# Raw W1 tiles loaded into later W2 places, and two weights' low parts subtracted on VectorE

## The chip, the cores and the metric

The kernel runs on one core of one Trainium2 chip. The metric is the device time of one execution in microseconds; the kernel before takes 933.64 us, the median of three runs (932.16 to 934.44). One more execution was profiled, and all rows of this document's first part come from it.

## The reference

Inputs are x (8 batches, 8 heads, 512 tokens, 64 features) and state (8, 8, 32, 64). Three stages follow each other.

```
a  = softmax(x @ state^T / 8);  xread = a @ state          # 512 rows a batch
a2 = softmax(state @ x^T / 8);  sread = a2 @ x             # 32 rows a batch
x1 = [xread ; sread], heads side by side                   # 8 x 544 x 512
x2 = x1 + relu(layernorm(x1) * g @ W1) @ W2                # W1 512x2048, W2 2048x512
out = (sigmoid(causal_conv5(x2)) * (x2 @ w_val)) @ w_out   # two weights of 512x512
```

The weights come as 64-bit floats and are turned into 32-bit ones on the chip.

## The kernel before, in words

**Precision.** A product of 32-bit numbers is made of three fp32r matmuls: each operand is split into a high part and a low part (`split_sb`, L72: ScalarE copies the high part at L73, and the engine given as an argument subtracts it from the source at L74), and `mm3` (L76 to L79) adds high by low, low by high and high by high. For the first four tiles of the hidden layer in batch 0 plain fp32 matmuls are used instead (L601, L639).

**Weights.** W1 is cut into 16 tiles `("1", j)`, four for each quarter q = j // 4 of the hidden layer, and W2 into 16 tiles `("2", f)`, one for each block of 128 hidden features. A raw tile is 128 x 512 numbers of 8 bytes, 4 KB in a partition. `load_raw` (L446 to L449) issues its DMA on SyncE's queue. `decode_a` (two ScalarE activations, L463 and L465) and `decode_b` (four VectorE instructions, L471, L473, L474, L478) make a 32-bit tile of it. A W2 tile, raw and later split into two parts, lives in a place of its own, `w2_0` to `w2_15`, 4 KB each. Raw W1 tiles go through four rotating buffers, `raw`, so a fifth can only be loaded when one of the first four has been decoded. The plain copies of W2 tiles 0 to 3 stand in the places w2_15 and w2_14 for a while, so the raw tiles 14 and 15 are loaded late (L814).

**Order.** TensorE's order is the program's. On ScalarE, VectorE, GpSimd and SyncE the order from about 28 us on is chosen when the kernel is built, by a scheduler that keeps its own reckoning of time: of the instructions that are ready by this reckoning it takes the one with the lowest priority number. The loads stand at the head of the program (L794 to L813) in the order W1 tiles 0 and 1, x of batch 0, W1 tiles 2 and 3, W2 tiles 0 and 1, state of batch 1, then `order[2:8]`, then x of batch 1 and so on. `order` (L783) is the order of decoding:

```
order = [("2", 0), ("2", 1), ("1", 4), ("2", 2), ("1", 5), ("1", 6), ("2", 3), ("1", 7)]
```

`share` (L947) deals the tiles of `order` out over the blocks f of the loop `segment` (L570): W1 tile 6 belongs to f = 2, W1 tile 7 and the four splits `("s", 0..3)` (L524, L525) to f = 3, W2 tiles 4 and 5 to f = 4. `behind` (L454) adds an edge of order: a tile that is dealt out at block f has its ScalarE part after the relu (L624) of block f - 1, and the splits `("s", j)` come after the last instruction of W1 tile 7.

**What W1 tiles 4 to 7 are for.** After the plain matmuls of block f = 3, TensorE makes the column sums of W1's second quarter: `colsum_parts(1)` (L156, eight matmuls, two for each of the W1 tiles 4 to 7), a ScalarE copy (L161), `colsum(1)` (L169), a copy (L170). Then `m_steps(0, 1)` (L138) multiplies the states by these W1 tiles, VectorE adds a correction (L144) and splits the result (L74), and from block 4 on the hidden layer is computed from that (`mm<-ahl,m`).

**The last phase's weights.** `prep_weights` (L773) loads, decodes and splits w_val during batch 2 (L896) and w_out while the state rows go through the hidden layer (L902), with `decode_split` (L484).

Of the kernel before, what the change touches and what calls it, by code (L numbers as in the profile page):

```python
# [44 lines left out]
def tile_kernel(ctx: ExitStack, tc: tile.TileContext, xT, xk, stT, sn, w1, w2, wval, wout, convw, gln, ident, out):  # L45
    nc = tc.nc
# [8 lines left out]
    def sb(shape, dt, tag, bufs=1):  # L55
        cnt[0] += 1
        return main.tile(shape, dt, tag=tag, bufs=BUFS.get(tag, bufs), name=f"{tag}_{cnt[0]}")
# [14 lines left out]
    def split_sb(hi, lo, src, eng):  # L72
        nc.scalar.activation(hi, src, AF.Copy)  # L73
        eng.tensor_tensor(lo, src, hi.bitcast(F32), op=ALU.subtract)  # L74
# [371 lines left out]
    def load_raw(tag, src):  # L446
        r = sb([P, DM, 2], U32, tag)
        nc.sync.dma_start(out=r, in_=src.bitcast(U32).rearrange("p (n two) -> p n two", two=2))
        return r  # L449
# [30 lines left out]
    def decode(r, c):  # L480
        decode_a(r, c)
        decode_b(r, c)

    def decode_split(tag, r):  # L484
        c = sb([P, DM], F32, "c")
        decode(r, c)
        hl = sb([P, 2, DM], F32R, tag)
        split_sb(hl[:, 0], hl[:, 1], c, nc.gpsimd)
        return hl

    raws, plain_w2 = {}, {}
# [281 lines left out]
    def prep_weights(src, dst, tags):  # L773
        for k in range(KT):
            raw = load_raw(tags[k], src[k * P:(k + 1) * P, :])
            dst[k] = decode_split(tags[k], raw)
            yield
# [9 lines left out]

    def load_tile(kind, j):
        if kind == "1":
            raws["1", j] = load_raw("raw", w1[j // 4, j % 4])  # L790
        else:
            raws["2", j] = load_raw(f"w2_{j}", w2[j * P:(j + 1) * P, :])

    load_tile("1", 0)  # L794
    load_state(0, nc.scalar)
    load_tile("1", 1)
    load_x(0)
    nc.scalar.dma_start(out=g_sb.rearrange("p k o -> p (k o)"), in_=gln)
    for j in range(2, KT):
        load_tile("1", j)  # L800
# [214 lines left out]
```

## Time and profile before

| | us |
|---|---|
| median of 3 runs | 933.64 |
| profiled execution | 934.39 |
| its span, first to last instruction | 932.6 |
| TensorE busy in it | 909.9 |
| VectorE / ScalarE / GpSimd busy | 579.5 / 375.7 / 191.8 |

The span is what the rows cover; 1.8 us of the profiled execution's time lies around it. TensorE is the engine with the least idle time, so what counts for the end is where it stands idle or runs at the lower of its two clock levels. Idle time on another engine matters only where TensorE waits for that engine.

### The profile page before, as it was taken

To read this page: it belongs to the slowest core of one execution; us is meant where nothing else is said; L and a number is where in the kernel's file an instruction comes from. 1 tells how busy PE (TensorE), PEld (TensorE's weight loads), DVE (VectorE), ACT (ScalarE), POOL (GpSimd) and SP (SyncE) were. 2 spreads that over 40 slices of the span, in tenths; PEclk is the share of its full clock that TensorE was granted. 3 is DMA by queue.
4 is the path that set the end of the run, shared out by engine and by line. 5 is a ranking of instruction groups with operands and counts; after the bars stand their busy time and mean duration, and the time that the engine had idled before them with its cause. 6 is when DMAs were issued, how large, how long until landed. Compare 5 with 4: busy or idle time off the path is not lost.

```text
span 932.6 us, 12963 instructions
## 1 busy us (share of the span) xinstructions
PE 909.9 (98%) x5152; PEld 688.8 (74%) x5152; DVE 579.5 (62%) x996; ACT 375.7 (40%) x688; POOL 191.8 (21%) x163
## 2 busy tenths in 40 slices
PE   7988999999999999999999999999999999999998
PEld 2336667777777677777777777777788988888886
DVE  6788898485275663435437245342349889988871
ACT  4745574243244342314224133231326555545532
POOL 0000010011312622411341141241202022333200
PEclk8979999999999999999999999999999999999999
DMA  9912320022012111110111110110112113222122
GB/s 361 355 55 105 101 72 1 1 93 96 1 49 95 71 48 49 49 44 6 49 48 45 49 46 1 24 49 1 46 57 79 53 40 126 100 92 91 46 89 69
DMA packets 26668, 66.45 MB, mean 71 GB/s; under 512 B 10864, under 2 KB 13040, under 8 KB 22512
## 3 DMA queue, kind: packets, MB, share of 16 engines
q1 hardware_dynamic: 25984, 65.24, 19.7%
q8 instruction: 40, 0.66, 0.3%
q10 hardware_dynamic: 624, 0.40, 0.2%
q14 instruction: 20, 0.16, 0.1%
HBM read 47.80 MB, written 17.83 MB: 70 GB/s over the span
## 4 chain that ended last, share of the span: by engine, by line
PE 90%; DVE 5%; DMA 2%; ACT 1%; issue 1%; SPq 0%; ACTq 0%; DVEq 0%
PE acc L77 16%; PE acc L79 15%; PE acc L78 15%; PE mm L77 9%; PE mm L79 8%; PE mm L78 8%; PE at L138 4%; PE at L77 2%; PE at L78 2%; PE at L79 2%; PE mm L913 1%; PE acc L639 1%; PE at L385 1%; DMA big<-in_xT 1%; PE mm L601 1%; PE at L276 1%
## 5 line engine op out<-in xcount | busy, mean ns | idle before, releaser
L626 DVE SCALAR_TENSOR_TENSOR hid<-mm,hid 128x512 fp32r<-128x512 f32 (+1 forms) x140 | 92.2, 659 | 211.7 <-ACT hid L624 211.6
L77 PE MATMUL acc<-hid,w 128*128 128x512 f32 (+1 forms) x560 | 213.5, 381 | 3.2 <-DVE hid L626 2.1
L79 PE MATMUL acc<-hid,w 128*128 128x512 f32 (+1 forms) x560 | 211.5, 378 | 0.0
L78 PE MATMUL acc<-hid,w 128*128 128x512 f32 (+1 forms) x560 | 211.2, 377 | 0.0
L624 ACT ACTIVATE hid<-mm 128x512 fp32r<-128x512 f32 (+2 forms) x144 | 82.5, 573 | 245.3 <-PE mm L79 240.8
L77 PEld LDWEIGHTS acc<-hid,w 128*128 128x128 f32 x560 | 105.4, 188 | 25.6 <-DVE hid L626 2.7
L77 PE MATMUL mm<-ahl,m 128*128 128x512 f32 (+1 forms) x312 | 121.2, 388 | 0.0
L79 PEld LDWEIGHTS acc<-hid,w 128*128 128x128 f32 x560 | 105.4, 188 | 20.0
L78 PEld LDWEIGHTS acc<-hid,w 128*128 128x128 f32 x560 | 105.4, 188 | 19.2
L78 PE MATMUL mm<-ahl,m 128*128 128x512 f32 (+1 forms) x312 | 115.3, 370 | 0.0
L79 PE MATMUL mm<-ahl,m 128*128 128x512 f32 (+1 forms) x312 | 115.3, 370 | 0.0
L74 POOL TENSOR_TENSOR m<-mb,m 128x512 fp32r<-128x512 f32 x48 | 65.4, 1378 | 201.9 <-ACT m L73 201.9
L702 DVE SCALAR_TENSOR_TENSOR ahl<-big,cw,ahl 128x511 f32<-128x511 f32 (+3 forms) x128 | 103.3, 851 | 0.4
L77 PEld LDWEIGHTS mm<-ahl,m 128*128 128x128 f32 x312 | 59.0, 189 | 40.3 <-issue 32.3
L73 ACT ACTIVATE m<-mb 128x512 fp32r<-128x512 f32 x62 | 39.0, 629 | 87.6 <-DVE mb L144 87.4
L79 PEld LDWEIGHTS mm<-ahl,m 128*128 128x128 f32 x312 | 59.0, 189 | 10.2
L78 PEld LDWEIGHTS mm<-ahl,m 128*128 128x128 f32 x312 | 59.2, 190 | 8.5 <-DVE m L74 0.5
L144 DVE SCALAR_TENSOR_TENSOR mb<-cs,sbn,at 128x512 f32<-128x512 f32 x62 | 43.5, 743 | 28.8 <-PE at L138 28.8
L688 POOL TENSOR_TENSOR w<-big,w 128x512 fp32r<-128x512 f32 x24 | 38.4, 1629 | 93.6 <-ACT w L686 77.0
L78 PE MATMUL acc<-w,raw 128*128 128x512 f32 (+1 forms) x144 | 54.3, 377 | 0.0
L79 PE MATMUL acc<-w,raw 128*128 128x512 f32 (+1 forms) x144 | 54.3, 377 | 0.0
L77 PE MATMUL acc<-w,raw 128*128 128x512 f32 (+1 forms) x144 | 54.3, 377 | 0.0
(173 smaller groups left out, 1330.2 us busy)
## 6 DMA issues: line engine op xcount, KB each, us to landing
raw<-in_w SPq DMA_DIRECT2D x16, 512.0 KB, 5.2
big<-in_xT SPq DMA_DIRECT2D x8, 1024.0 KB, 5.2
w<-in_w SPq DMA_DIRECT2D x16, 512.0 KB, 9.4
big<-in_xk SPq DMA_DIRECT2D x8, 1024.0 KB, 5.7
x2d<-x SPq DMA_DIRECT2D x8, 1024.0 KB, 4.0
big<-x2d SPq DMA_DIRECT2D x8, 1024.0 KB, 4.9
out<-hid SPq DMA_DIRECT2D x16, 512.0 KB, 2.8
raw<-in_wval SPq DMA_DIRECT2D x4, 512.0 KB, 3.5
```

The source lines that it names most:

```text
L73: nc.scalar.activation(hi, src, AF.Copy)
L74: eng.tensor_tensor(lo, src, hi.bitcast(F32), op=ALU.subtract)
L77: nc.tensor.matmul(acc, lhsT=wh, rhs=xl, start=first, stop=False)
L78: nc.tensor.matmul(acc, lhsT=wl, rhs=xh, start=False, stop=False)
L79: nc.tensor.matmul(acc, lhsT=wh, rhs=xh, start=False, stop=last)
L138: nc.tensor.matmul(mp[u][32 * p:32 * p + 32, :], lhsT=stg[r, p, :], rhs=w1s[4 * q + p][r], start=True, stop=True)
L144: a = nc.vector.scalar_tensor_tensor(mb, cs[:, q], sbn[:, u], mp[u], op0=ALU.mult, op1=ALU.add)
L276: nc.tensor.matmul(sr[r, u, :], lhsT=a2T[u][:, c, r], rhs=xn[:, c, 2 * p + u, :], start=(c == 0), stop=(c == 3))
L624: marks["act"] = nc.scalar.activation(hid[:, 0], h, AF.Relu)
L626: marks["dve"] = nc.vector.scalar_tensor_tensor(hid[:, 1], h, 0.0, hid[:, 0].bitcast(F32), op0=ALU.max, op1=ALU.subtract)
L688: nc.gpsimd.tensor_tensor(lo, src, hi.bitcast(F32), op=ALU.subtract)
L702: t = nc.vector.scalar_tensor_tensor(g[:, j:], x[:, :n - j], cw_sb[:, k, PAD - j:TAPS - j], g[:, j:], op0=ALU.mult, op1=ALU.add)
```

## The change

Raw W1 tiles 4 to 7 are loaded into the places of W2 tiles 10 to 13 and no longer into the four `raw` buffers. The loads of W2 tiles 10 to 13 then use these places after W1 tiles 4 to 7 have been decoded, and W1 tiles 8 to 11 take over the `raw` buffers from tiles 0 to 3. In `decode_split` the subtraction that makes the low part of a tile of w_val and w_out goes from GpSimd to VectorE: eight instructions of 128 x 512.

```diff
         hl = sb([P, 2, DM], F32R, tag)
-        split_sb(hl[:, 0], hl[:, 1], c, nc.gpsimd)
+        split_sb(hl[:, 0], hl[:, 1], c, nc.vector)
         return hl
 ...
         if kind == "1":
-            raws["1", j] = load_raw("raw", w1[j // 4, j % 4])
+            tag = f"w2_{j + 6}" if j // 4 == 1 else "raw"
+            raws["1", j] = load_raw(tag, w1[j // 4, j % 4])
         else:
             raws["2", j] = load_raw(f"w2_{j}", w2[j * P:(j + 1) * P, :])
```

## Rows read from the trace of the kernel before

**Rows 1.** The page: busy us (share of the span) x instructions of each engine.

```profile
PE 909.9 (98%) x5152; PEld 688.8 (74%) x5152; DVE 579.5 (62%) x996; ACT 375.7 (40%) x688; POOL 191.8 (21%) x163
```

**Rows 2.** Waits of TensorE: who waited for whom, us in total, times, longest.

```profile
PE at L156 <- DVE w L478: 4.7, 1, 4.7
...
PE at L138 <- ACT t L245: 1.8, 1, 1.8
...
PE acc L77 <- DVE x L312: 1.1, 1, 1.1
```

**Rows 3.** Busy time by stretch: PE, PEld, DVE, ACT, POOL, clock, DMA share, GB/s.

```profile
14.00:28.00 14.00, 14.00 (x64) 5.64 (x63) 13.65 (x34) 7.91 (x17) 0.00 (x0) 0.97 1.02 413
...
45.50:50.10 4.60, 0.00 (x0) 0.00 (x0) 2.21 (x5) 2.86 (x6) 0.00 (x0) 0.87 0.25 100
50.10:57.40 7.30, 6.59 (x21) 1.12 (x21) 7.24 (x14) 1.74 (x3) 0.00 (x0) 0.50 0.45 144
57.40:61.40 4.00, 4.00 (x14) 1.79 (x9) 3.81 (x6) 1.93 (x4) 0.00 (x0) 0.78 0.00 0
...
100.00:140.00 40.00, 38.41 (x242) 27.23 (x242) 39.93 (x83) 25.41 (x47) 3.35 (x1) 1.00 0.26 84
```

**Rows 4.** Timeline of TensorE: start, us, instruction, count, idle before and releaser.

```profile
44.35 1.06 PE L156 MATMUL at<-w,g 128*32 128x512 f32 x6
...
63.18 0.40 PE L77 MATMUL mm<-ahl,m 128*128 128x512 f32 x1
```

**Rows 5.** Timeline of ScalarE, 44 to 53 us, and one row of 108 us.

```profile
44.46 0.60 ACT L624 ACTIVATE hid<-mm 128x512 f32<-128x512 f32 x1 [2.22 <-PE mm L601]
44.95 0.66 ACT L463 ACTIVATE c<-w 128x512 f32<-128x512 f32 x1
...
47.15 0.64 ACT L463 ACTIVATE w<-raw 128x512 f32<-128x512 f32 x1
...
52.09 0.59 ACT L161 COPY t<-at 128x512 f32<-128x512 f32 x1 [3.73 <-PE at L156]
...
108.31 0.66 ACT L463 ACTIVATE c<-w 128x512 f32<-128x512 f32 x1
```

**Rows 6.** Timeline of VectorE, 41 to 64 us.

```profile
41.70 0.43 DVE L471 TENSOR_SCALAR w<-w 128x512 f32<-128x512 f32 x1 [1.81 <-ACT w L463]
...
47.82 0.43 DVE L471 TENSOR_SCALAR w<-w 128x512 f32<-128x512 f32 x1 [3.86 <-ACT w L463]
...
60.11 1.29 DVE L74 TENSOR_TENSOR m<-mb,m 128x512 fp32r<-128x512 f32 x2
63.38 2.48 DVE L367 TENSOR_TENSOR t<-x,at 128x512 f32<-128x512 f32 x4 [1.99 <-PE at L79]
```

**Rows 7.** SyncE's queue: start, us from first to last issue, DMA, count.

```profile
17.33 10.42 SPq L448 DMA_DIRECT2D w<-in_w  x7
...
30.05 9.18 SPq L448 DMA_DIRECT2D raw<-in_w  x4
```

**Rows 8.** DMA issues between 30.0 and 30.2 us: count, KB each, us to landing.

```profile
raw<-in_w SPq DMA_DIRECT2D x1, 512.0 KB, 10.4
```

**Rows 9.** Busy time in the stretches where w_val and w_out are decoded.

```profile
290.00:313.00 23.00, 21.87 (x121) 16.02 (x120) 19.23 (x27) 11.15 (x21) 13.92 (x10) 1.00 0.29 104
700.00:720.00 20.00, 17.93 (x147) 17.52 (x146) 17.85 (x30) 13.09 (x27) 6.15 (x6) 1.00 0.22 79
```

**Rows 10.** Groups by line and shape, whole span: count | busy us, mean ns | idle before.

```profile
L474 DVE TENSOR_SCALAR raw<-raw 128x512 uint16<-128x512 uint16 x20 | 16.6, 832 | 0.3
...
L74 DVE TENSOR_TENSOR w<-c,w 128x512 fp32r<-128x512 f32 x12 | 8.2, 690 | 0.2 <-ACT w L73 0.2
L74 POOL TENSOR_TENSOR w<-c,w 128x512 fp32r<-128x512 f32 x4 | 5.8, 1452 | 11.3 <-ACT w L73 11.3
L74 POOL TENSOR_TENSOR raw<-c,raw 128x512 fp32r<-128x512 f32 x4 | 5.2, 1294 | 5.0 <-ACT raw L73 5.0
```

**Rows 11.** The same for VectorE between 288 and 314 us.

```profile
L474 DVE TENSOR_SCALAR raw<-raw 128x512 uint16<-128x512 uint16 x4 | 4.7, 1187 | 0.3
```

## The prediction, made before the change was run

> **What bounds the kernel now.** The page comes first: TensorE is busy 909.9 us of a span of 932.6 [rows 1], so 22.7 us are idle, and only those, and what runs at the lower clock, can be won. The list of TensorE's waits says where: the longest single wait is 4.7 us, at L156 on VectorE's L478, the last instruction of a weight's decode [rows 2]. The timeline places it: six of the eight column-sum matmuls run at 44.35, and the last two start only at about 50.1 [rows 4], because W1 tile 7 is not decoded. The busy times by stretch give the second price: TensorE does nothing from 45.5 to 50.1, and afterwards its granted clock is 0.50 from 50.1 to 57.4 (the lower level, 1.2 GHz) and 0.78 on average to 61.4 [rows 3]. Half of 6.59 busy us and 0.22 of 4.00 are 3.3 + 0.9 = 4.2 us lost to the clock. With the 4.6 idle before, 8.8 us hang on this place; with the short wait for L161 behind it (0.7, what 50.1 to 57.4 holds beside the 6.59 busy) it is 9.5.
>
> Why is tile 7 late? SyncE's queue shows seven W2 loads from 17.33 on, and the four raw W1 loads only from 30.05 [rows 7]; the first of these took 10.4 us to land [rows 8]. By the order of decoding that is W1 tile 6 (two raw W1 loads went before), so it was in place at 40.5, and tile 7, the next, at about 41. W1 tiles 4 to 7 want buffers that W1 tiles 0 to 3 still hold, and the scheduler lets loads with a free place pass them. VectorE shows the effect: idle 1.81 us before 41.70 and 3.86 us before 47.82, both for ScalarE's L463, which opens the decode of tiles 6 and 7 [rows 6]. ScalarE itself stood idle for 2.22 us before the relu at 44.46, then did four instructions for W2 tiles 4 and 5, and took tile 7 at 47.15 [rows 5]. So the last stretch of the delay is the order chosen at build time, by a reckoning in which tile 7 lands late; the 41 us above is when it really landed.
>
> **The change part by part.** *Places.* W2 places 10 to 13 are free from the start, so the loads of W1 tiles 4 to 7 need no wait and go out in program order. Up to and with W1 tile 7 that is twelve weight tiles of 0.524 MB, x at 1.05 MB and some 0.26 MB of small loads: 7.6 MB. At the 413 GB/s of the stretch 14 to 28 [rows 3] it takes 18.4 us, so tile 7 lands near 20 us instead of 41. That hides both idle times of VectorE. The tile's ScalarE part may then follow the relu of block f = 2 and not that of f = 3, and fits into the 2.22 idle us.
>
> What starts next is bounded in two ways. First by VectorE: its work up to the low parts of m, which end at 61.40 (60.11 + 1.29), is the same, less the 1.81 + 3.86 = 5.67 us of idling: 55.7. The hidden layer's block 4 then starts at 55.7 and not at 63.18 [rows 4], a gain of 7.4. Second by ScalarE: if the four instructions for W2 tiles 4 and 5, which have the better priority, still go ahead of the copy L161, this copy comes at 47.15 instead of 52.09 [rows 5]. If all behind it keeps its pace, low clock included (2.4 us of idling stay), the gain is 4.9. The upper end is the 9.5 from above, if L161 goes first and the correction L144 is put ahead of W2's decode. I take 6.2, the middle of 4.9 and 7.4: the ScalarE order is the one the rows show, but a shorter pause should give back some of the clock.
>
> What is late next: VectorE, which works without a pause right behind this place, so that the 1.8 us wait at L138 for L245 [rows 2] stays and moves along. From 100 to 140 us VectorE is busy 39.93 of 40 us while TensorE is 38.41 [rows 3]. Both come to this stretch earlier by the same amount, so I cost it at nothing; if VectorE gained less than TensorE, the 1.6 idle us of TensorE there would grow by the difference, at most the 7.4 - 4.9 = 2.5 us between the two bounds.
>
> *Waits added.* The loads of W2 tiles 10 to 13 now wait for the decode of W1 tiles 4 to 7, and W1 tiles 8 to 11 for tiles 0 to 3. Behind these on SyncE's queue stand x and keys of batch 1, later W1 tiles and states. The last of the decodes ends by about 45; a load takes 10.4 us when the queues are full, so W2 tile 13 is there by 56 at the latest. The next W2 tiles after 7 go through ScalarE at 108.31 [rows 5], so 50 us cover it: 0. Were this cover gone, each tile would cost up to 10.4.
>
> *Low parts on VectorE.* Eight subtractions of 690 ns go to VectorE, 5.5 us, and eight leave GpSimd, 5.2 + 5.8 = 11.0 us [rows 10]. Four lie between 290 and 313, where VectorE has 23 - 19.23 = 3.8 us free, four between 700 and 720 with 2.15 free [rows 9]; each group needs 2.8. For w_val the bounds are -1.1 (the wait at L312 [rows 2], should a VectorE that GpSimd slows less arrive earlier) and +2.8 (all four ahead of an instruction TensorE waits for). For w_out they are 0, as TensorE has no such wait there, and +2.8. I take 0 for both, the row of idle time being nearest: the free time or the end of GpSimd's interference holds them, and the tiles are not used before the last phase.
>
> In the stretch of w_val GpSimd is busy 13.92 of 23 us [rows 9], and VectorE's L474 takes 1187 ns on average against 832 over all twenty [rows 10, 11], so the two engines do slow each other. The Trainium skill, "SBUF — State Buffer", section "Who interferes with whom", speaks against the edit: a VectorE instruction with two SBUF inputs and a GpSimd instruction that reads SBUF exclude each other, and the later waits in full. The moved subtraction has two SBUF inputs, and batch 2's other GpSimd work stays, so by this rule each of the four could take 0.7 + 1.3 = 2.0 us as an estimate, 8.0 in all, against 2.8 by the rows; as the four GpSimd instructions that go blocked VectorE in turn, both sums net out near 0 for TensorE.
>
> *Sum.* 934.39 - 6.2 + 0 = 928.2 for the profiled execution; it lies 0.75 above the median of 933.64, so the median goes to 927.4.
>
> **The rivals.** *The order stays.* If the scheduler keeps tile 7 behind the relu at 44.46, it takes at best the slot of 44.95 instead of 47.15 [rows 5]: 2.2 us less, 931.4, a quarter of a per cent. For it: the delay's last stretch was order, not landing. Against it: tile 7 has the better priority, and 2.22 idle us lie open before that relu. This is also the case in which the loads come early and nothing uses it.
>
> *All of it comes back.* L161 first, full clock, no pause: 9.5, 924.1. Against it: VectorE's work allows 7.4 unless its order changes too.
>
> *Slower.* The moved subtraction waits on VectorE for ScalarE's high part, with the relu's low part (L626) queued behind it and TensorE waiting for that. Between decode and the high part's end lie 0.6 to about 3 us, as ScalarE's place for it is also chosen by a reckoning. At 1.5 us for each of eight places, with nothing hidden, it is 12 us, less 6.2: +5.8, 939.4; from 0.8 us a place on it eats the gain, from 1.2 the kernel is slower beyond what can be told. For it: VectorE has under 4 us free in either stretch [rows 9]. Against it: the twelve W2 splits already done this way had 0.2 us of idling in all before them, for ScalarE [rows 10].
>
> **How the numbers follow.** A measurement of this kernel tells 0.3%, 2.8 us, from no change. The forecast (gain 4.9 to 7.4, less or more by up to 1 for the second edit) has 0.55, all of it back 0.16, the order stays 0.18, slower 0.11. The order's 931.4 is within 0.3%. So faster 0.71, same 0.18, slower 0.11. The likeliest case reaches from 925.2 to 929.8; the range takes in the 924.1 case with a little room and the order's: 923.5 to 933.0, leaving out the slower case and the ends of the others.
>
> **What would show it.** Right: raw W1 loads 4 to 7 leave SyncE before 20 us; VectorE has no idle time over 1 us between 28 and 46; the wait of L156 on L478 is gone; a shorter one at L169 on L161 stands in its place, the clock's low stretch is shorter, and block 4's first `mm<-ahl,m` starts near 57. The stretches 290 to 313 and 700 to 720, moved by about 6 us, keep TensorE's idle time. Wrong: L463 of tile 7 still follows the relu of f = 3; the shift at block 4 is there but gone by 160 us, which would mean that VectorE's full stretch sets the end; or new waits of TensorE on L626 in the two late stretches.

## The result and the profile after

The changed kernel takes 925.47 us, the median of four runs (925.15 to 925.79), against 934.04 for the kernel before: 8.57 us less, a ratio of 0.9909 with a 95% interval of 0.9893 to 0.9926. Its profiled execution took 925.42 us with a span of 923.6. Forecast were 927.4, in a range of 923.5 to 933.0.

The list of TensorE's waits of the changed kernel, the answer to [rows 2]. The 4.7 us at L156 have become 0.3; a wait of 1.1 at L169 and one of 0.8 before block 4 stand in their place.

```profile
PE at L138 <- ACT t L245: 2.0, 1, 2.0
PE acc L77 <- DVE x L312: 1.8, 2, 1.4
...
PE at L169 <- ACT t L161: 1.1, 1, 1.1
PE at L77 <- DVE mb L144: 0.8, 1, 0.8
...
PE at L156 <- DVE w L478: 0.3, 1, 0.3
```

The queues and engines around that place, one fence each. SyncE's queue, against [rows 7]: six loads leave in one go from 9.19, among them W1 tiles 4 to 7, and the last two land 7.5 us after their issue (second fence), so tile 7 is there by 22.3 and not by 41.

```profile
9.19 5.57 SPq L448 DMA_DIRECT2D w<-in_w  x6
```

```profile
w<-in_w SPq DMA_DIRECT2D x2, 512.0 KB, 7.5
```

ScalarE, against [rows 5]: tile 7 (L463 at 42.52) now stands ahead of the relu of 44.27 and right behind that of 42.04; the four instructions for W2 tiles 4 and 5 still go ahead of the copy L161.

```profile
42.04 0.58 ACT L624 ACTIVATE hid<-mm 128x512 f32<-128x512 f32 x1
42.52 0.66 ACT L463 ACTIVATE w<-w 128x512 f32<-128x512 f32 x1
...
44.27 0.60 ACT L624 ACTIVATE hid<-mm 128x512 f32<-128x512 f32 x1 [0.49 <-PE mm L601]
44.76 0.68 ACT L463 ACTIVATE c<-w 128x512 f32<-128x512 f32 x1
...
47.03 0.57 ACT L161 COPY t<-at 128x512 f32<-128x512 f32 x1
```

VectorE, against [rows 6]: one idle time of 1.80 is left of two that summed to 5.67.

```profile
43.21 0.43 DVE L471 TENSOR_SCALAR w<-w 128x512 f32<-128x512 f32 x1 [1.80 <-ACT w L463]
...
55.57 1.35 DVE L74 TENSOR_TENSOR m<-mb,m 128x512 fp32r<-128x512 f32 x2
56.84 2.48 DVE L367 TENSOR_TENSOR t<-x,at 128x512 f32<-128x512 f32 x4
```

TensorE, against [rows 4], and the clock, against [rows 3]: block 4 starts at 56.43 and not at 63.18, and the stretch behind the column sums runs at a granted clock of 1.00 where it was 0.50.

```profile
45.54 1.05 PE L156 MATMUL at<-w,g 128*32 128x512 f32 x2 [0.32 <-DVE w L478]
47.65 1.12 PE L169 MATMUL at<-t,part 128*128 128x512 f32 x2 [1.06 <-ACT t L161]
...
56.43 0.40 PE L77 MATMUL mm<-ahl,m 128*128 128x512 f32 x1
```

```profile
47.60:54.90 7.30, 6.52 (x26) 2.05 (x26) 7.14 (x15) 1.82 (x3) 0.00 (x0) 1.00 0.32 105
```

To see where the rest came from, TensorE's order being that of the program, the start of the same matmul is subtracted in two timelines. The table gives this lead over the kernel before, in us, for its profiled execution and those of all runs below. A column names a matmul and its time in the kernel before: the first of the column sums, the first of batch 1's scores (L189), and L385, which recurs through the whole run.

| | column sums, 44 | scores of batch 1, 68 | L385, 93 | L385, 143 | L385, 300 | L385, 380 | L385, 691 | L385, 741 |
|---|---|---|---|---|---|---|---|---|
| changed kernel | 0.19 | 6.74 | 6.79 | 8.07 | 8.06 | 7.34 | 7.34 | 8.96 |
| x1_places | 0.61 | 7.01 | 8.45 | 9.42 | 9.46 | 9.47 | 9.47 | 9.80 |
| x2_low | 0.49 | 0.80 | 0.80 | 1.36 | 1.35 | 0.65 | 0.65 | 1.94 |
| x3_wout | 0.37 | 6.73 | 8.23 | 9.50 | 9.49 | 9.51 | 9.51 | 11.30 |
| x4_fill | 0.47 | 3.99 | 2.88 | 3.91 | 3.90 | 3.92 | 3.92 | 4.93 |
| x5_two | -0.57 | 5.99 | 5.93 | 7.12 | 7.18 | 7.19 | 7.19 | 7.17 |
| x6_order | 0.60 | 3.79 | 1.25 | 2.51 | 2.46 | 2.47 | 2.48 | 2.45 |
| x7_share | -0.48 | 7.50 | 4.55 | 5.59 | 5.64 | 5.63 | 5.63 | 6.93 |
| x8_fill2 | 0.21 | 6.59 | 8.05 | 9.04 | 9.03 | 9.02 | 9.02 | 11.20 |
| x9_after | 0.31 | 6.69 | 6.55 | 7.82 | 7.83 | 7.12 | 7.13 | 8.99 |
| x10_wout | -1.21 | 5.34 | 5.38 | 6.64 | 6.66 | 6.67 | 6.67 | 8.01 |
| x11_x1d | 0.36 | 1.43 | 2.42 | 3.68 | 3.67 | 3.66 | 3.67 | 3.69 |
| x12_copies | 0.47 | 6.87 | 8.34 | 9.59 | 9.58 | 8.96 | 8.96 | 10.36 |

For the changed kernel it reads: +6.55 at W1 tile 7, +1.28 between 93 and 143, -0.72 where w_val is decoded, +1.62 where w_out is. The 9.0 of the spans are these four and the 0.2 of the start.

### The profile page after: what moved, and what is told of

It reads as the page before. It is cut to its first block, busy times and chain, and to the rows that moved or that the text cites. A ratio compares the mean times of both kernels' runs of the same rounds, so it can differ in the third digit from the quotient of the medians.

```text
span 923.6 us, 12956 instructions
## 1 busy us (share of the span) xinstructions
PE 905.1 (98%) x5151; PEld 687.6 (74%) x5152; DVE 579.0 (63%) x1004; ACT 374.7 (41%) x688; POOL 179.8 (19%) x155
## 4 chain that ended last, share of the span: by engine, by line
PE 89%; DVE 5%; ACT 3%; DMA 2%; issue 1%; SPq 0%; ACTq 0%; DVEq 0%
PE acc L77 16%; PE acc L79 16%; PE acc L78 16%; PE mm L77 9%; PE mm L79 8%; PE mm L78 8%; PE at L138 4%; PE at L77 2%; PE at L78 2%; PE at L79 2%; PE mm L914 1%; PE at L276 1%; PE at L385 1%; DMA big<-in_xT 1%; PE at L262 1%
## 5 line engine op out<-in xcount | busy, mean ns | idle before, releaser
L626 DVE SCALAR_TENSOR_TENSOR hid<-mm,hid 128x512 fp32r<-128x512 f32 (+1 forms) x140 | 92.3, 659 | 210.1 <-ACT hid L624 210.0
L702 DVE SCALAR_TENSOR_TENSOR ahl<-big,cw,ahl 128x508 f32<-128x508 f32 (+3 forms) x128 | 102.8, 852 | 0.2
L144 DVE SCALAR_TENSOR_TENSOR mb<-cs,sbn,at 128x512 f32<-128x512 f32 x62 | 43.5, 743 | 28.3 <-PE at L138 27.5
```

The lines of the kernel that those rows point to most:

```text
L144: a = nc.vector.scalar_tensor_tensor(mb, cs[:, q], sbn[:, u], mp[u], op0=ALU.mult, op1=ALU.add)
L626: marks["dve"] = nc.vector.scalar_tensor_tensor(hid[:, 1], h, 0.0, hid[:, 0].bitcast(F32), op0=ALU.max, op1=ALU.subtract)
L702: t = nc.vector.scalar_tensor_tensor(g[:, j:], x[:, :n - j], cw_sb[:, k, PAD - j:TAPS - j], g[:, j:], op0=ALU.mult, op1=ALU.add)
```

## The experiments

Each was timed beside the kernel before on the same chip.

| | median us | runs | ratio to before, 95% interval |
|---|---|---|---|
| x1_places | 926.53 | 6 | 0.9930 (0.9914 to 0.9947) |
| x2_low | 932.40 | 12 | 0.9989 (0.9974 to 1.0004) |
| x3_wout | 923.08 | 4 | 0.9896 (0.9880 to 0.9911) |
| x4_fill | 929.42 | 5 | 0.9963 (0.9949 to 0.9977) |
| x5_two | 926.41 | 5 | 0.9921 (0.9909 to 0.9933) |
| x6_order | 933.30 | 12 | 0.9987 (0.9974 to 1.0001) |
| x7_share | 927.27 | 5 | 0.9929 (0.9916 to 0.9942) |
| x8_fill2 | 924.26 | 4 | 0.9896 (0.9883 to 0.9909) |
| x9_after (the changed kernel) | 925.58 | 6 | 0.9919 (0.9898 to 0.9940) |
| x10_wout (x3_wout) | 924.72 | 6 | 0.9907 (0.9885 to 0.9929) |
| x11_x1d | 931.11 | 12 | 0.9985 (0.9968 to 1.0002) |
| x12_copies | 924.54 | 6 | 0.9912 (0.9889 to 0.9935) |

**The two edits apart.** x1_places leaves `decode_split` on GpSimd:

> Only the places of the raw W1 tiles 4 to 7 are changed; the low parts of w_val and w_out stay on GpSimd. Theory P (the places carry nearly all of the gain): the profile keeps the lead of 8.1 us that the changed kernel had at the column sums of batch 2 (6.55 from W1 tile 7, 1.34 from the writes of x1 that leave earlier, 0.2 from the start) up to the end, so about 8 us under the kernel before: 926. Theory L (the subtractions matter as much): it is 2 us or more slower than the changed kernel, 927.5 or above.

x2_low is the other half, the kernel before with `nc.vector` in `decode_split`:

> Only the eight subtractions go to VectorE; the places stay as before. Theory P: a loss of 0.7 us near 310 (w_val, TensorE waits longer for the copy at L312) and a gain of 1.6 near 715 (w_out, TensorE's wait of 1.75 for L626 goes), 0.9 us in all: 933.1. Theory L: 2 us or more, 932 or below. The prediction's own term was 0, 934.0.

Measured are 6.9 us for the places (933.40 to 926.53) and about 1.0 for the subtractions, whose interval reaches 1. x1_places keeps its lead between L385 at 300 and 380, and x2_low loses 0.70 there and gains 1.29 from 691 to 741, much as the changed kernel does (-0.72 and +1.62). Theory P holds. About 0.3 of the 1.62 is not the subtractions' doing: x1_places, which has them on GpSimd, gains 0.33 there, and x4_fill (below), which has them there too, even 1.01.

x3_wout takes the better half of the second edit:

```diff
-        split_sb(hl[:, 0], hl[:, 1], c, nc.vector)
+        split_sb(hl[:, 0], hl[:, 1], c, nc.gpsimd if tag == "raw" else nc.vector)
```

> Places changed, w_out's four subtractions on VectorE, w_val's four left on GpSimd. If the w_val part costs 0.7 us, this one is 0.7 us faster than the changed kernel: 924.8, TensorE's waits on L312 near 303 sum to 1.1 and not to 1.8. If that loss was chance of one execution, it is the same, 925.5.

923.08, more than expected. The lead over 300 to 380 no longer falls, which is w_val's 0.7; another 1.5 us come between the scores of batch 1 and L385 at 93, where the code is the same. x9_after and x10_wout are the two kernels again, on one chip:

> The changed kernel once more, beside the version with w_val's low parts on GpSimd. If the difference between the two so far (925.5 against 923.1) was w_val's 0.7 us and for the rest chance between occasions, it now lies within 1.2 us of that version; if w_val's subtractions cost more than the 0.7 that the traces show, the difference stays above 2.

> Places changed, w_out on VectorE, w_val on GpSimd, once more: 0.7 us faster than the changed kernel on the same chip, by w_val; 2 us or more faster if the earlier difference was real.

Now it is 925.58 against 924.72, 0.86 apart. So the difference is w_val's 0.7 (0.72, 0.70 and 0.71 in three executions), the rest was chance. The mean granted clock of the timed executions fits that: 0.998 in all four of x3_wout, but in only one of four of the changed kernel and two of six of x10_wout, with 0.994 to 0.996 in the others. x3_wout is the fastest version tried, but by less than the runs of one kernel spread (922.89 to 926.40 in x10_wout).

**Where that chance lies.** All versions with new places but x7_share and x8_fill2 pause for 2.0 us at L138, waiting for L245, near 67. Busy time by stretch of the pause and of what follows: first the changed kernel, then x3_wout, then x10_wout, which is the same program.

```profile
66.70:68.70 2.00, 0.03 (x1) 0.00 (x0) 2.00 (x7) 0.81 (x3) 0.00 (x0) 1.00 0.63 252
68.70:76.00 7.30, 7.28 (x34) 4.28 (x35) 7.30 (x17) 4.32 (x9) 0.00 (x0) 0.77 0.02 7
```

```profile
66.50:68.50 2.00, 0.25 (x2) 0.00 (x0) 2.00 (x7) 0.59 (x2) 0.00 (x0) 1.00 0.53 203
68.50:74.60 6.10, 5.87 (x34) 3.75 (x35) 6.10 (x14) 4.57 (x11) 0.00 (x0) 1.00 0.04 13
```

```profile
68.00:70.10 2.10, 0.15 (x1) 0.00 (x0) 2.10 (x6) 0.79 (x3) 0.00 (x0) 1.00 0.52 192
70.10:77.60 7.50, 7.46 (x36) 4.38 (x36) 7.50 (x18) 4.52 (x9) 0.00 (x0) 0.77 0.01 5
```

Behind the same pause the clock fell to 0.77 or stayed at 1.00; 0.23 of 7.3 us are 1.7, about the 1.5 seen. In the seven profiled executions with this pause it fell in four (the changed kernel, x9_after, x10_wout, x5_two) and stayed in three (x1_places, x3_wout, x12_copies). x8_fill2 puts matmuls of no use into the pause of x3_wout:

```diff
+                if unit == (1, 0):
+                    idle = ps(ps_mm, "mm", [P, S])
+                    for _ in range(8):
+                        nc.tensor.matmul(idle, lhsT=warm[:, :P], rhs=warm, start=True, stop=True)
                 m_steps(*unit)
```

> The faster version so far with 8 bf16 matmuls of no use, 1.9 us, in TensorE's pause of 2.0 us at L138 (waiting for L245, near 67). In the changed kernel's profile the clock fell to 0.77 behind this pause, in that of the version with w_out alone it stayed at 1.00. If the fall after such a short pause is a matter of chance, filling it takes the chance away: clock 1.00 behind it in the profile, and the timed runs lie within 0.5 us of each other at the lower end, 922.8 to 923.3. Rival: the spread of runs has another cause and stays; the fill delays the waiting matmuls by 0.2 and nothing is won: 923.3 or above.

Its profile shows the lead without the fall (8.05 at L385, 93), but the four runs lie between 923.18 and 924.88. Their granted clocks are 0.998 in the two faster and 0.994 in the two slower, so in these the clock fell somewhere all the same; where, no trace shows. The pause is one source of the spread and not the only one. The start is another: the table's first column goes from -1.21 to 0.61. The late first x of x10_wout (10.4 us, 9.1 in the kernel before) is part of that, and the clock behind its arrival another. x1_places and x5_two get x at 9.63 and 9.59, and their stretches from 10 to 20 us are

```profile
10.00:20.00 10.00, 10.00 (x50) 3.78 (x35) 9.90 (x25) 6.96 (x15) 0.50 (x1) 0.88 1.03 404
```

```profile
10.00:20.00 10.00, 9.95 (x43) 3.62 (x29) 9.90 (x24) 6.21 (x13) 0.17 (x1) 0.73 1.04 406
```

that is, a clock of 0.88 against 0.73, and a lead of 0.61 against -0.57 at the column sums; 0.15 of 10 us are 1.5, about the 1.2 between them. A gain by x8_fill2 is not shown.

**The clock behind the long wait.** x4_fill is the kernel before with 20 such matmuls ahead of the last of the column sums (q is the quarter, k the W1 tile in it):

```diff
+            idle = at_ps([P, S]) if q == 1 else None
             for k in range(KT):
+                if q == 1 and k == KT - 1:
+                    for _ in range(20):
+                        nc.tensor.matmul(idle, lhsT=warm[:, :P], rhs=warm, start=True, stop=True)
```

> The kernel before with 20 bf16 matmuls of no use, 4.6 us, put between the sixth and the seventh of the column-sum matmuls, into TensorE's idle time. Clock theory: the granted clock stays at 1.00 after the wait, and the 4.2 us that the low clock cost come back as far as VectorE lets them: block 4 starts about 2 us earlier (VectorE's low parts of m end near 61 whatever TensorE does), 932. Rival: TensorE's slow instructions there were waiting for something else, and nothing moves, 934. If the low clock alone set the pace, 4.2, 929.8.

Busy time by stretch of x4_fill, for the same stretches as [rows 3]:

```profile
45.50:50.10 4.60, 4.24 (x19) 1.71 (x18) 2.63 (x5) 2.45 (x5) 0.00 (x0) 1.00 0.17 69
50.10:57.40 7.30, 6.62 (x29) 2.08 (x27) 7.30 (x15) 2.09 (x4) 0.00 (x0) 1.00 0.45 144
```

The decode is as late as before, but the clock stays at 1.00, and the lead grows by 3.5 us to the scores of batch 1. TensorE's timeline puts all of it in the clock: from the last column sums on its matmuls take less time, and from 52.5 to block 4 at 59.19 it waits for nobody. That is more than the 2 expected, which VectorE was to cap. VectorE's order changed, the low parts of W2 tiles 4 and 5 (two instructions of 0.6 each) going behind those of m, which so end at 59.5; in the old order they would have ended 1.2 later, and TensorE would have had to wait. So the fall of the clock was a cost beside the wait. That VectorE caps what comes back did not show in this run. In time the fill gives 4.0 us (933.40 to 929.42), a gain between 93 and 143 among them.

**Which tiles, and load or order.** x5_two moves two tiles only:

```diff
-            tag = f"w2_{j + 6}" if j // 4 == 1 else "raw"
+            tag = f"w2_{j + 6}" if j in (6, 7) else "raw"
```

> Only W1 tiles 6 and 7 go to W2 places (12 and 13), 4 and 5 stay in the raw buffers, the subtractions on GpSimd. Theory A (only these two tiles were late, and only tile 7 held TensorE): as with all four, block 4 starts 6.5 us earlier than in the kernel before, total 926. Theory B (the whole order of the loads matters, tiles 4 and 5 too): block 4 gains clearly less, 5 or under, 928 or above.

Block 4 starts at 57.19 in an execution that is 0.57 late at the column sums; the lead grows by 6.56 from there to the scores, as with four tiles. Theory A holds: tiles 4 and 5 needed no other place.

x6_order leaves all loads and places and deals W2 tiles 4 and 5 out later:

```diff
-        share[0] = iter([1, 2, 2, 5, 2, 1, 1, 0] + [1, 2] * 4 + [1] * 8)
+        share[0] = iter([1, 2, 2, 5, 0, 3, 1, 0] + [1, 2] * 4 + [1] * 8)
```

> The kernel before with W2 tiles 4 and 5 dealt out one block later (f = 5), so that ScalarE takes W1 tile 7 straight behind the relu at 44.46; its load and its place stay as before. Theory order (the tile had landed by about 41 and ScalarE's order kept it back): L463 of tile 7 starts at 45.0 with no wait for a DMA, the column sums end 2.2 us earlier, and with less work ahead of m on VectorE block 4 starts 5 us earlier or more; 928 to 931. Theory landing (the load was the cause): L463 waits for the DMA until 47 and the total stays within 1 us of the kernel before.

ScalarE in x6_order, around tile 7 (L463 at 44.35, no idle time before it):

```profile
43.86 0.60 ACT L624 ACTIVATE hid<-mm 128x512 f32<-128x512 f32 x1 [2.06 <-PE mm L601]
44.35 0.67 ACT L463 ACTIVATE w<-raw 128x512 f32<-128x512 f32 x1
```

The waits of TensorE in it:

```profile
PE acc L78 <- DVE w L74: 4.0, 1, 4.0
PE at L156 <- DVE w L478: 2.6, 1, 2.6
```

The first half of the order theory holds: the tile had landed by 44.35, and only the order had kept it back to 47.15. The column sums end 2.25 us earlier and block 4 starts at 59.39. Its total is wrong: the split of a W2 tile put off is late itself, TensorE waits 4.0 us for it, and 933.30 remain. Order alone does not pay here; the early load lets tile 7 be decoded in ScalarE's idle time and pushes nothing back.

x7_share tries the same on x3_wout, with W2 tile 5 only (`[1, 2, 2, 5, 1, 2, 1, 0]`):

> Places changed and w_out on VectorE (the faster version so far, 923.1), with W2 tile 5 dealt out at block 5 and not 4, so that the copy L161 comes two ScalarE instructions earlier and VectorE has 2.4 us less ahead of m. If TensorE's waits at L169 (1.06) and before block 4 (0.77) are set by these, up to 1.8 us are won at block 4: 921.3. Rival: VectorE has no idle time up to 90 us, the work only moves and the wait at L138 for L245 grows by what was won: 923.1, or above if the clock falls there.

The wait of TensorE at L138 for L245 and what follows, in its timeline and stretches:

```profile
71.58 2.63 PE L138 MATMUL at<-w,stg 64*32 64x512 f32 x16 [5.61 <-ACT t L245]
```

```profile
71.50:80.00 8.50, 8.41 (x38) 5.13 (x39) 8.50 (x20) 5.36 (x11) 0.00 (x0) 0.68 0.00 0
```

The rival holds: up to the scores it gained 1.4 us more than the changed kernel (7.98 from the column sums on, against 6.55), and the wait behind grew from 2.0 to 5.6 with a fall of the clock. That is 3.6 us, more than was won: on VectorE, busy without a pause there, the instruction that L245 waits for (L244) now starts at 70.58, behind more of VectorE's other work, and not at 67.67 as in x3_wout. VectorE and its order set this stage.

**The gain between 93 and 143.** In the kernel before VectorE stood idle at L653 for a buffer that batch 0's writes of x1d had still to read:

```profile
98.83 0.69 DVE L653 TENSOR_TENSOR t<-acc,t 128x512 f32<-128x512 f32 x1 [1.19 <-DMA x1d<-t]
```

x11_x1d is the kernel before with the load of W1 tile 12 kept behind these writes on SyncE's queue by an added edge of order (the loads of W1 tiles 12 to 15 stand in the program behind `sread(0)`):

```diff
-    for o in order[24:26] + order[20:24]:
+    for o in order[24:26]:
 ...
         sread(0)
+        for o in behind_x1d:
+            load_tile(*o, after="x1d")
```

> The kernel before with one thing changed on SyncE's queue: the load of W1 tile 12 stands behind batch 0's x of batch 2 and the four writes of x1d, not ahead of them; the order on all other engines is as before. If the 1.34 us that the changed kernel gained between 97 and 114 come from that order (VectorE's idle 1.19 us at L653, waiting for the x1d writes to read their buffer), this gains 1.0 to 1.4 at the transposes L262 of batch 2: 933. If they come from something else, nothing moves there, 934.

SyncE's queue, first in the kernel before, then in x11_x1d:

```profile
89.26 0.33 SPq L448 DMA_DIRECT2D raw<-in_w  x1
89.68 0.93 SPq L107 DMA_DIRECT2D big<-in_xT  x1
90.71 2.15 SPq L282 DMA_DIRECT2D x1d<-t  x4
```

```profile
86.25 0.33 SPq L107 DMA_DIRECT2D big<-in_xT  x1
88.34 1.76 SPq L282 DMA_DIRECT2D x1d<-t  x4
90.20 0.38 SPq L448 DMA_DIRECT2D raw<-in_w  x1
```

With the load of W1 tile 12 at the head, which waits for its buffer, x of batch 2 and the writes left late and then shared the engines. In x11_x1d the idle time at L653 is gone and the lead grows by 1.3 from L385 at 93 to 143; x6_order and x4_fill leave all loads in their places, and yet the scheduler put x and the first two of the four writes ahead of that load, as it did in the changed kernel; they gain 1.3 and 1.0 without idle time at L653. x2_low, with the order of before, waits 0.5 and gains 0.6. So the gain comes from this order, and the new places are not needed for it. The time of x11_x1d, 931.11, has an interval that reaches 1, so the trace and not the time shows it. (Its other leads, up to 93, come from stretches with the low clock.)

**The copies near 303.** x12_copies is x3_wout with `if k % 2 and b != 3` in `x1_group`:

> The version with w_val on GpSimd, and the two VectorE copies L312 of batch 3 given to ScalarE. TensorE waits 1.1 us for them near 303, behind decode instructions that GpSimd slows. If that wait goes and no other takes its place, 1.1 us faster than that version. Rival: ScalarE's copies, now four in a row among decode and splits, are late in turn, and TensorE waits as long for L314: no gain.

The rival holds: TensorE waits 2.0 us for ScalarE's copies instead of 1.1, and the lead falls by 0.6 there.

```profile
PE acc L77 <- ACT x L314: 2.0, 1, 2.0
```

## Why the prediction was right, and where its sizes were off

*The mechanism.* Raw W1 tiles 4 to 7 left SyncE before 15 us, tile 7 landed at about 22 (20 was forecast) and was decoded ahead of the relu of block 3, and L161 stayed behind the four W2 instructions. Measured from the column sums on, L161 comes 4.9 us earlier (52.09 to 47.03, less 0.19): the ScalarE bound, as forecast. Behind L161 the matmuls up to block 4 take 2.5 us less at the full clock, and 0.8 of that goes into the new wait for L144. Together this is 6.6 at block 4 (56.43). The term was 6.2; it measured 6.55 up to the scores of batch 1, and x1_places, which has only this edit, shows 6.40. That "a shorter pause should give back some of the clock" was right, and too careful: the pauses of 0.3 and 1.1 left the clock at 1.00.

The VectorE bound was misread, and that the result lies between the two bounds is in part luck. The bound lets block 4 start when VectorE has the low parts of m. In the kernel before these end at 61.40, block 4 starts 1.8 us later, and TensorE's rows up to it show no wait behind the one for L161:

```profile
52.73 2.08 PE L169 MATMUL at<-t,part 128*128 128x512 f32 x2 [0.68 <-ACT t L161]
54.73 2.70 PE L138 MATMUL at<-w,stg 64*32 64x512 f32 x16
57.37 4.58 PE L639 MATMUL acc<-hid,w 128*128 128x512 f32 x8
61.38 0.80 PE L77 MATMUL at<-ahl,sbhl 128*128 128x512 f32 x1
```

So TensorE itself, mostly at the low clock, set block 4's start, and VectorE then waited 1.99 us for it at L367 [rows 6]. Nor did VectorE lose all its 5.67 us of idling: 1.80 stayed, as tile 7's ScalarE part came only behind the relu of 42.04, against the sign of no idle time over 1 us. The low parts of m end at 56.92, 4.5 us earlier and not 5.7.

*Behind it.* That the wait at L138 stays and moves along held (2.0). That the lead passes the full VectorE stretch from 100 to 140 unchanged did not: 1.28 came on top. The prediction costed SyncE's queue at 0 by looking at what the moved loads wait for, and not at what stands behind a load that waits; that a raw W1 load held back x1d's writes is the term it missed, and x11_x1d shows it. As x4_fill and x6_order got this gain with no load moved, that the change brought it was luck of the order chosen at build time.

*The second edit.* Forecast was 0 with bounds; in the changed kernel's profile it measured -0.72 and +1.62. For w_out the step that failed is the sentence that TensorE has no such wait there. It has: the list of its waits in the kernel before holds a row that the prediction left out, and the timeline puts it at 715.83.

```profile
PE acc L77 <- DVE hid L626: 2.1, 2, 1.7
```

```profile
715.83 0.39 PE L77 MATMUL acc<-hid,w 128*128 128x256 f32 x1 [1.74 <-DVE hid L626]
```

There VectorE's L474 took 1.82 us beside a subtraction on GpSimd, and the relu's low part (at 715.36) stood behind it:

```profile
713.37 1.82 DVE L474 TENSOR_SCALAR w<-w 128x512 uint16<-128x512 uint16 x1
```

```profile
713.17 1.42 POOL L74 TENSOR_TENSOR w<-c,w 128x512 fp32r<-128x512 f32 x1 [1.47 <-ACT w L73]
```

With the subtractions on VectorE, one wait of 0.73 is left:

```profile
704.01 0.39 PE L77 MATMUL acc<-hid,w 128*128 128x256 f32 x1 [0.73 <-DVE hid L626]
```

For w_val the bound of +2.8 was the right side. VectorE around the copies L312 in the changed kernel, while GpSimd is busy from 295.1 to 304.0:

```profile
296.77 1.44 DVE L74 TENSOR_TENSOR raw<-c,raw 128x512 fp32r<-128x512 f32 x1
298.14 1.39 DVE L144 SCALAR_TENSOR_TENSOR mb<-cs,sbn,at 128x512 f32<-128x512 f32 x2
299.45 1.47 DVE L471 TENSOR_SCALAR c<-c 128x512 f32<-128x512 f32 x1
300.85 1.82 DVE L474 TENSOR_SCALAR raw<-raw 128x512 uint16<-128x512 uint16 x1
302.47 0.71 DVE L312 COPY x<-acc 128x512 f32<-128x512 f32 x1
```

The subtraction that falls into GpSimd's other work takes 1.44 us, where the other three, with GpSimd idle, take 0.69 each, and it pushes the rest back. By the rule of the Trainium skill, "SBUF — State Buffer", section "Who interferes with whom", that was to be expected of two SBUF inputs beside a GpSimd instruction that reads SBUF; the trace agrees for this one of the four and shows 0.75 us of blocking, less than the estimate of 1.3.

*The rivals.* "The order stays" did not happen, and x6_order shows what a better order alone was worth: 2.25 us at the column sums, as the 2.2 of that case, but not in time (933.30). "Slower", by subtractions that hold L626 up, fell: the two waits on L626, 1.74 and 0.33, became one of 0.73. "All of it comes back" (924.1) lies nearer to the measured 925.47 than the forecast of 927.4 does, but not by its mechanism: L161 did not go first, and the 9.0 us between the profiled executions are 6.55, three small terms and the 0.2 of the start.

## What to carry to other kernels

In this kernel a load that waited for a buffer cost in two ways: its own tile was late, and on SyncE's queue so was what stood behind it. A place that stays free until later in the kernel took away the first; the second went with the order of the queue, which the scheduler also changed where no load had moved. The scheduler orders by its own reckoning of when a load lands, so the earlier load was also an earlier place in ScalarE's order. A wait can also hide what is behind it: count the engine's own rows up to the next start before putting that start down to another engine. And the same subtraction gained on VectorE where GpSimd then fell silent, and lost where GpSimd stayed busy.

## What the runs showed of the hardware

- Behind a pause of TensorE of 4.7 us the granted clock was 0.50 for the next 7.3 us; with 20 matmuls of no use in that pause (x4_fill) it stayed at 1.00.
- After one and the same pause of TensorE of 2.0 us the granted clock fell to 0.77 for the next 7 us in some executions of a program (x10_wout) and stayed at 1.00 in another (x3_wout). This moved single executions by about 1.5 us, more than the second edit is worth.
- TensorE's wait for the first x ended between 8.9 and 10.4 us over the executions, and the granted clock from 10 to 20 us was 0.70 to 0.90. Late arrival and low clock together cost x10_wout 1.2 us at the column sums, and it carried them to the end.
- Beside GpSimd instructions on 128 x 512 tiles VectorE's L474 took 1.82 us (at 713 in the kernel before, at 300 in the changed one), where it took 0.75 with GpSimd idle (at 287 in the changed kernel).
